# The first 20 microseconds of a GEGLU feed-forward kernel: another order of chunks, two blocks of x transposed by TensorE, and constant matmuls until x lands

## The chip, the cores and the metric

The kernel runs on one core of one Trainium2 chip. The metric is the device time of one execution in microseconds (us). "The span" is the time from the first to the last instruction in the profile, about 1.8 us shorter than the device time.

PE is TensorE, DVE is VectorE, ACT is ScalarE and POOL is GpSimd; SP only issues DMAs here. A q behind a name (SPq, ACTq, PEq) marks the part of the engine that issues its instructions. PSUM is the memory that the matmuls here write to. A constant matmul multiplies constants and its result is thrown away: it only keeps TensorE busy.

Differences here are at most about one per cent, and the rounds ran on different chips, so ratios are taken inside the same rounds. A ratio is the mean time of one kernel's runs over the mean time of the other's runs of the same rounds, so it is not quite the ratio of the medians that are quoted.

## The reference

```
def reference(x, w_gate, w_up, w_down):          # all bfloat16
    return (gelu_tanh(x @ w_gate) * (x @ w_up)) @ w_down
# x: 32*32 = 1024 tokens x 1024;  w_gate, w_up: 1024 x 3584;  w_down: 3584 x 1024
```

Contraction over 1024 is eight blocks of 128 (k = 0 to 7). The 3584 gate and up columns are 28 chunks of 128 (m). The 1024 tokens are two halves of 512 (h). One matmul takes a 128x128 weight block and 512 tokens, and a finished (m, h) pair needs eight of them for gate and eight for up, in two PSUM banks. The eight banks (the program's tile `ps`, 128x8x512) hold four pairs at a time. Work on "one block k" in the head is therefore eight matmuls, in both kernels.

## The kernel before

A small list scheduler writes instructions to each engine in program order and waits for exactly what each one needs. So the order inside one engine's list matters: an engine that waits holds up all that stands behind it in its own list, DMA issues included. The head, abridged:

```
# SP: all of x, transposed by DMA, one 1024x128 block per DMA
for k in range(DK):
    pr.add("sp", "dma_start_transpose", xT[:, k:k + 1, :], xf[:, k * P:(k + 1) * P], w=[("x", k)], dma=f"x{k}")
# ACT: gate and up weights of chunks 0 and 1, two blocks k per DMA (rows of 512 bytes)
for k in range(0, DK, 2):
    load_w("act", "g", 0, k, k + 2)
    load_w("act", "u", 0, k, k + 2)
for i in range(22):                              # constant matmuls, before x lands
    pr.add("pe", "matmul", ps[:, 7, 0:P], scr[:, :], scr[:, :], start=True, stop=True, r=["scr"], w=[("ps", 7)])
# ... further weight loads on SP and ACT ...
KO = DK - 2
units = [(m, h) for m in range(2) for h in range(2)]     # 2 chunks x 2 token halves = 8 banks
for k in range(KO):                              # contraction outermost
    for kind in ("g", "u"):
        for i, (m, h) in enumerate(units):
            mm_gu(kind, m, h, k, 2 * i + (kind == "u"))
# ... blocks 6 and 7 pair by pair, each followed by GELU and the product;
# ... then chunks 2 to 27 one pair at a time, then the down projection (not touched)
```

## Time and profile before

| | before |
|---|---|
| median device time, three runs | 303.19 us |
| span | 301.6 us |
| TensorE (PE) busy | 293.9 us, 97% |
| chain of work that ended last | 94% PE |
| first real matmul starts | 5.84 us |
| 49th real matmul (first one of block 6) starts | 19.21 us |

TensorE bounds the kernel, and what it loses before its last matmul it loses nearly all in the head; copying and storing the last piece, 2.4 us, is not touched. The chain that ended last has the steady rate. Its columns are start, length, and what it was:

```profile
5.67 8.30 DMA xT<-in_x_dram
...
14.02 0.82 PE ps L98 x3
...
14.89 10.74 PE ps L98 x49
...
25.68 10.74 PE ps L98 x49
```

Fifty matmuls of 512 columns take 10.79 us (14.89 to 25.68), 0.216 us each, and it goes on like that until the half-width matmuls of the down projection. The line says x49 because about one record in fifty is missing in this trace: it has 439 of the 448 gate matmuls. Before that, the chain runs through a transposing DMA of x, issued at 5.67 us and landed at 13.97: the fourth block.

A useful yardstick is the start of the 49th real matmul. Without any loss it would start at 48 x 0.2158 = 10.36 us. Whatever it starts later than that is the loss of the head: here 19.21 - 10.36 = 8.85 us.

The timeline of the head shows how the loss arises. Its columns are start, length, engine and instruction, count, and in brackets the idle time before with what ended it. Length includes the tail of the last matmul, and the idle time counts only from the end of that tail, so rates and waits are read from the starts:

```profile
1.00 2.53 PE L98 MATMUL ps<-scr 128*128 128x128 bf16 x22 [1.00 <-POOL scr L98]
...
5.84 1.87 PE L98 MATMUL ps<-xT,wg 128*128 128x512 bf16 x4 [2.32 <-DMA xT<-in_x_dram]
...
7.50 1.91 PE L98 MATMUL ps<-xT,wu 128*128 128x512 bf16 x4
...
9.21 1.51 PE L98 MATMUL ps<-xT,wg 128*128 128x512 bf16 x4
...
10.56 1.03 PE L98 MATMUL ps<-xT,wu 128*128 128x512 bf16 x4
...
11.51 1.02 PE L98 MATMUL ps<-xT,wg 128*128 128x512 bf16 x4
...
14.02 0.82 PE L98 MATMUL ps<-xT,wg 128*128 128x512 bf16 x3 [0.62 <-DMA xT<-in_x_dram]
...
19.21 0.59 PE L98 MATMUL ps<-xT,wg 128*128 128x512 bf16 x2
```

There is a hole from 3.5 to 5.84 us. After it four matmuls take 1.7 us (0.43 us each, half rate) until about 10.3 us, then 0.86 us. A wait for x ends at 14.02. (The trace has three of the four matmuls there.) The last line is the 49th matmul.

One more line is needed for the argument, the group of x's transposing DMAs (duration of the issue: least, median and greatest, in ns):

```profile
L98 SPq DMA_TRANSPOSE xT<-in_x_dram x8: 1235/1358/3987, 0.7 to 15.2; - x8
```

### The profile page before, as it was taken

How to read it: one execution, taken by the hardware profiler on the slowest of the kernel's cores; microseconds unless marked ns; L12 is line 12 of the kernel's file. 1: busy time of each engine (PE TensorE's matmuls, PEld its weight loads, DVE VectorE, ACT ScalarE, POOL GpSimd, SP SyncE). 2: the span in 40 equal slices, each digit the busy share in tenths (PEclk: the TensorE clock that was granted, in tenths of full speed). 3: DMA queues.
4: the chain of work that ended last, by engine and by line, in shares of the span. 5: the costliest groups of instructions: out<-in, count | busy, mean ns of one | idle time of the engine just before them, and what ended most of it. 6: DMA issues, size and time to landing. Idle time of an engine off the chain costs nothing.

```text
span 301.6 us, 3132 instructions
## 1 busy us (share of the span) xinstructions
PE 293.9 (97%) x1368; PEld 136.8 (45%) x1394; DVE 43.8 (15%) x64; ACT 40.1 (13%) x67; POOL 0.4 (0%) x5
## 2 busy tenths in 40 slices
PE   5999999999999999999999999999999999999996
PEld 3344444444444444444444444444444444444455
DVE  0022211112111122111121111220000000000000
ACT  1022112111112111121111211110000000000000
POOL 0000000000000000000000000000000000000000
DMA  8999460302905705603021030000000100010001
GB/s 161 252 254 350 146 230 11 131 0 83 332 4 176 245 0 194 225 9 133 0 86 56 0 139 2 0 0 17 20 17 17 37 17 17 17 37 17 17 17 37
DMA packets 31341, 26.41 MB, mean 88 GB/s; under 512 B 9184, under 2 KB 27744, under 8 KB 31328
## 3 DMA queue, kind: packets, MB, share of 16 engines
q1 hardware_dynamic: 28112, 24.64, 26.5%
q10 hardware_dynamic: 3216, 1.57, 2.4%
q8 instruction: 11, 0.18, 0.3%
q14 instruction: 2, 0.02, 0.0%
HBM read 22.02 MB, written 2.10 MB: 80 GB/s over the span
## 4 chain that ended last, share of the span: by engine, by line
PE 94%; DMA 3%; SPq 2%; issue 1%; ACT 0%
PE ps L98 94%; DMA xT<-in_x_dram 3%; SPq L98 2%; ACT xT L98 0%
## 5 line engine op out<-in xcount | busy, mean ns | idle before, releaser
L98 PE MATMUL ps<-xT,wg 128*128 128x512 bf16 x439 | 107.2, 383 | 3.4 <-DMA xT<-in_x_dram 2.9
L98 PE MATMUL ps<-xT,wu 128*128 128x512 bf16 x439 | 106.9, 381 | 0.5
L98 PE MATMUL ps<-wd,hT 128*128 128x512 bf16 (+1 forms) x468 | 96.5, 366 | 0.4
L98 PEld LDWEIGHTS ps<-xT,wg 128*128 128x128 bf16 x448 | 44.0, 99 | 57.1 <-issue 4.6
L98 PEld LDWEIGHTS ps<-wd,hT 128*128 128x128 bf16 x476 | 46.6, 98 | 50.4
L98 PEld LDWEIGHTS ps<-xT,wu 128*128 128x128 bf16 x448 | 44.0, 98 | 53.5 <-issue 1.1
L98 DVE TENSOR_TENSOR hT<-g,ps 128x512 bf16<-128x512 f32 x56 | 38.5, 688 | 164.6 <-PE ps L98 164.6
L98 ACT ACTIVATE g<-ps 128x512 f32<-128x512 f32 x56 | 33.4, 597 | 165.6 <-PE ps L98 165.6
L98 DVE CAST xT<-ps 128x512 bf16<-128x512 f32 (+1 forms) x8 | 5.3, 658 | 88.1 <-PE ps L98 88.1
L98 ACT ACTIVATE xT<-ps 128x512 bf16<-128x512 f32 (+1 forms) x9 | 5.2, 573 | 93.1 <-PE ps L98 93.1
L98 PE MATMUL ps<-scr 128*128 128x128 bf16 x22 | 2.5, 313 | 1.0 <-POOL scr L98 1.0
L98 PEld LDWEIGHTS ps<-scr 128*128 128x128 bf16 x22 | 2.3, 147 | 1.0 <-POOL scr L98 1.0
L98 ACT ACT_TABLE_LOAD x1 | 1.3, 1283 | 0.7 <-PEq L276 0.7
L98 ACT ACTIVATE warm<-const-float32-0.0 128x1 f32<-128x1 f32 x1 | 0.2, 203 | 0.0
L98 POOL MEMSET scr<- 128x128 bf16 x1 | 0.2, 204 | 0.3 <-POOLq L276 0.3
L276 POOL MEMSET const-bfloat16-1.0<- 128x1 bf16 x1 | 0.1, 102 | 0.0
L276 POOL MEMSET const-uint8-127<- 128x1 uint8 x1 | 0.1, 101 | 0.0
L276 POOL MEMSET const-float32-0.0<- 128x1 f32 x1 | 0.1, 98 | 0.2 <-issue 0.2
L276 POOL MEMSET const-float32-1.0<- 128x1 f32 x1 | 0.1, 98 | 0.0
## 6 DMA issues: line engine op xcount, KB each, us to landing
wd<-in_w_down_dram SPq DMA_DIRECT2D x7, 1024.0 KB, 5.2
wg<-in_w_gate_dram SPq DMA_DIRECT2D x6, 1024.0 KB, 7.7
wu<-in_w_up_dram SPq DMA_DIRECT2D x6, 1024.0 KB, 10.6
out_dram<-xT SPq DMA_DIRECT2D x15, 128.0 KB, 1.7
wg<-in_w_gate_dram ACTq DMA_DIRECT2D x4, 128.0 KB, 5.1
wu<-in_w_up_dram ACTq DMA_DIRECT2D x4, 128.0 KB, 6.1
wu<-in_w_up_dram ACTq DMA_DIRECT2D x1, 512.0 KB, 8.1
wg<-in_w_gate_dram SPq DMA_DIRECT2D x1, 512.0 KB, 5.0
```

The lines of the kernel that those rows point to most:

```text
L98: ins = getattr(eng, name)(*args, **kw)
L276: nc = _bacc.Bacc("TRN2", target_bir_lowering=False, num_devices=1)
```

## The change

Its intent is to start real work earlier, to need less transposed x per block, and to have TensorE at full rate by then.

- The first eight banks hold four chunks by one token half, instead of two chunks by two halves. A block k then needs 512 tokens of x (128 KB instead of 256) and 256 KB of weights (instead of 128), in rows of 1 KB instead of 512 bytes.
- Blocks 0 and 1 of the first token half come by one plain DMA and are transposed by TensorE, and are copied from PSUM by VectorE and ACT.
- All other x still comes by transposing DMA, in 14 halves of 512 tokens.
- The constant matmuls start earlier and are longer, to last until x lands.

```
+        xn = sb("xn", [P, 4, 2 * P], BF16)
-        groups = [(0, 2, 0, 0), (2, 2, 0, 2)]      # then groups of 4 chunks
+        groups = [(c, min(GW, FM - c), (c // GW) % NWB, 0) for c in range(0, FM, GW)]
+        # identity for the transposes: memset and affine_select on POOL
+        for n in [512] * 7 + [128] * 4:
+            pr.add("pe", "matmul", ps[:, 3, 0:n], one[:, 0:P], one[:, 0:n], start=True, stop=True, w=[("ps", 3)])
+        NX = 2
+        pr.add("sp", "dma_start", xn[:, :, :], x_r[:, 0:4, 0:NX * P], w=["xn"], dma="xn")
-        for k in range(DK):
-            pr.add("sp", "dma_start_transpose", xT[:, k:k + 1, :], xf[:, k * P:(k + 1) * P], ...)
+        for h in range(2):
+            for k in range(NX if h == 0 else 0, DK):
+                pr.add("sp", "dma_start_transpose", xT[:, k:k + 1, h * 512:(h + 1) * 512], ...)
+        for k in range(NX):
+            load_w("act", "g", 0, k, k + 1)
+            load_w("act", "u", 0, k, k + 1)
+        for k in range(NX):
+            for i, b in enumerate((6, 7) if k == 0 else (4, 5)):
+                half = ps[:, b, 0:P].bitcast(BF16)
+                for t in range(2):
+                    pr.add("pe", "transpose", half[:, t * P:(t + 1) * P], xn[:, 2 * i + t, k * P:(k + 1) * P], ident[:, :], ...)
+                dst = xT[:, k, i * 256:(i + 1) * 256]
+                if i == 0:
+                    pr.add("dve", "tensor_copy", dst, half, ...)
+                else:
+                    pr.add("act", "activation", dst, half, ACTF.Copy, ...)
-        for k in range(0, DK, 2):
+        for k in range(NX, DK, 2):
             load_w("act", "g", 0, k, k + 2)
             load_w("act", "u", 0, k, k + 2)
-        # 22 constant matmuls of 128 columns; 2 x 2 pairs with contraction outermost
+        # per token half: 4 chunks, contraction outermost, last two blocks chunk by chunk
 ... (the rest follows from the new groups)
```

More of the change, by code (lines that the diff above doesn't have):

```diff
@@ L120, in bass_standalone__geglu_ffn__sampling_kernel @@
     out_r = of.rearrange("(tc p) d -> p tc d", p=P)
+    x_r = xf.rearrange("(tc p) d -> p tc d", p=P)
     wg_r = w_gate.rearrange("(dk p) f -> p dk f", p=P)
@@ L140, in bass_standalone__geglu_ffn__sampling_kernel @@
         warm = sb("warm", [P, 2], FP32)
-        scr = sb("scr", [P, P], BF16)
+        ident = sb("ident", [P, P], BF16)
+        xn = sb("xn", [P, 4, 2 * P], BF16)
         osb = xT
@@ L144, in bass_standalone__geglu_ffn__sampling_kernel @@
         const0 = nc.const_aps.tensor(0.0, [P, 1], FP32)
-        groups = [(0, 2, 0, 0), (2, 2, 0, 2)]
-        c, j = 4, 1
-        while c < FM:
-            n = min(GW, FM - c)
-            groups.append((c, n, j % NWB, 0))
-            c, j = c + n, j + 1
+        groups = [(c, min(GW, FM - c), (c // GW) % NWB, 0) for c in range(0, FM, GW)]
         where = {}
@@ L170, in mm_gu @@
                 start=(k == 0), stop=(k == DK - 1),
-                r=[(kind, buf, slot, k), ("x", k)], w=[("ps", bank)])
+                r=[(kind, buf, slot, k), ("x", k, h)] + ([("x", k, "b")] if h == 0 else []), w=[("ps", bank)])
         glu_n = [0]
@@ L181, in glu @@
                 r=[("gb", g), ("ps", bu)], w=[("h", m, h)])
-        pr.add("pool", "memset", scr[:, :], 1.0, w=["scr"])
-        pr.add("act", "activation", warm[:, 0:1], const0, ACTF.Gelu_apprx_tanh)
-        for k in range(DK):
-            pr.add("sp", "dma_start_transpose", xT[:, k:k + 1, :], xf[:, k * P:(k + 1) * P], w=[("x", k)], dma=f"x{k}")
-        for k in range(0, DK, 2):
+        one = nc.const_aps.tensor(1.0, [P, 512], BF16)
+        pr.add("pool", "memset", ident[:, :], 0.0, w=["id0"])
@@ new lines, in bass_standalone__geglu_ffn__sampling_kernel @@
+        pr.add("pool", "affine_select", ident[:, :], ident[:, :], [[-1, P]], ALU.not_equal, 1.0,
+               base=0, channel_multiplier=1, r=["id0"], w=["ident"])
+        for n in [512] * 7 + [128] * 4:
[4 more added lines that the diff above has]
+            for k in range(NX if h == 0 else 0, DK):
+                pr.add("sp", "dma_start_transpose", xT[:, k:k + 1, h * 512:(h + 1) * 512],
+                       xf[h * 512:(h + 1) * 512, k * P:(k + 1) * P], w=[("x", k, h)], dma=f"x{k}_{h}")
@@ new lines, in bass_standalone__geglu_ffn__sampling_kernel @@
+        pr.add("act", "activation", warm[:, 0:1], const0, ACTF.Gelu_apprx_tanh)
+        for k in range(NX):
[5 more added lines that the diff above has]
+                for t in range(2):
+                    pr.add("pe", "transpose", half[:, t * P:(t + 1) * P], xn[:, 2 * i + t, k * P:(k + 1) * P],
+                           ident[:, :], r=["xn", "ident"], w=[("ps", b)])
+                dst = xT[:, k, i * 256:(i + 1) * 256]
+                if i == 0:
+                    pr.add("dve", "tensor_copy", dst, half, r=[("ps", b)], w=[("x", k, 0)])
+                else:
+                    pr.add("act", "activation", dst, half, ACTF.Copy, r=[("ps", b)], w=[("x", k, "b")])
@@ L189, in bass_standalone__geglu_ffn__sampling_kernel @@
+        for k in range(NX, DK, 2):
             load_w("act", "g", 0, k, k + 2)
             load_w("act", "u", 0, k, k + 2)
-        NDUMMY = 22
-        for i in range(NDUMMY):
-            pr.add("pe", "matmul", ps[:, 7, 0:P], scr[:, :], scr[:, :], start=True, stop=True,
-                   r=["scr"], w=[("ps", 7)])
-        load_w("sp", "g", 1)
-        load_w("act", "u", 1)
-        load_w("sp", "g", 2)
-        load_w("sp", "u", 2)
-        KO = DK - 2
-        units = [(m, h) for m in range(2) for h in range(2)]
@@ L203, in bass_standalone__geglu_ffn__sampling_kernel @@
-        for k in range(KO):
-            for kind in ("g", "u"):
-                for i, (m, h) in enumerate(units):
-                    mm_gu(kind, m, h, k, 2 * i + (kind == "u"))
-        for i, (m, h) in enumerate(units):
-            for kind, b in (("g", 2 * i), ("u", 2 * i + 1)):
-                for k in range(KO, DK):
-                    mm_gu(kind, m, h, k, b)
-            glu(m, h, 2 * i, 2 * i + 1)
+        KO = 2
+        for h in range(2):
+            steps = []
+            for m in range(4):
+                steps += [(m, kind, k) for kind in "gu" for k in range(KO)] if h else []
+            for k in range(KO if h else 0, DK - KO):
+                steps += [(m, kind, k) for kind in "gu" for m in range(4)]
+            for m in range(4):
+                steps += [(m, kind, k) for kind in "gu" for k in range(DK - KO, DK)] + [(m, None, None)]
+            for m, kind, k in steps:
+                if kind is None:
+                    glu(m, h, 2 * m, 2 * m + 1)
+                else:
+                    mm_gu(kind, m, h, k, 2 * m + (kind == "u"))
@@ L214, in bass_standalone__geglu_ffn__sampling_kernel @@
+        for gi in range(1, 3):
+            load_w("sp", "g", gi)
+            load_w("sp", "u", gi)
         wd_pieces = [(a, min(FM, a + 4)) for a in range(0, FM, 4)]
         loaded = 2
-        u = 4
-        for m in range(2, FM):
+        u = 8
+        for m in range(4, FM):
             for h in range(2):
@@ L250, in bass_standalone__geglu_ffn__sampling_kernel @@
                 pr.add("act", "activation", osb[:, tc, col:col + n], ps[:, b, 0:n], ACTF.Copy,
-                       r=[("ps", b)], w=[("o", ji), ("x", tc)])
+                       r=[("ps", b)], w=[("o", ji), ("x", tc, 0), ("x", tc, 1), ("x", tc, "b")])
             else:
                 pr.add("dve", "tensor_copy", osb[:, tc, col:col + n], ps[:, b, 0:n],
-                       r=[("ps", b)], w=[("o", ji), ("x", tc)])
+                       r=[("ps", b)], w=[("o", ji), ("x", tc, 0), ("x", tc, 1), ("x", tc, "b")])
             pr.add("sp", "dma_start", out_r[:, tc, col:col + n], osb[:, tc, col:col + n],
```

## The prediction

> **What bounds the kernel now.** TensorE. The page has PE busy 97%; the chain of waits is 94% PE. In steady state the chain runs 10.79 us per 50 matmuls of 512 columns, 0.216 us each. The work is 896 + 420 such matmuls and 56 of half width, 1344 in all: 290.0 us. The last PE step ends at 299.2, so about 9 us are lost, all at the head. Copying and storing the last piece, 2.4 us, does not change.
>
> The timeline shows that loss: (a) no real matmul until 5.84 us, when the first transposing DMA (1024x128, issued at 0.74) lands; the 22 small constant matmuls ended at 3.5 and PE idled 2.3 us; (b) from 5.84 to 10.3 matmuls start 0.43 us apart, half rate: 2.2 us lost; (c) waits for the third and fourth x block, until 11.5 and 14.0, about 1.2 us. Transposed blocks land at about 5.8, 8.4, 11.4 and 14.0; the work on one takes 8 x 0.216 = 1.73 us at full rate, so x by DMA alone, beside the weights, comes too slowly.
>
> [...] the spacing halves at 10.3, 4.5 us after PE became busy for good.
>
> **What the change does.**
> - x of contraction blocks 0 and 1 (first 512 tokens) comes as one plain 256 KB DMA. With first packets at about 2.05 us and 190 to 285 GB/s shared with block 0's weights, I estimate landing at 4.0 to 4.3 us.
> - Eight TensorE transposes and four PSUM copies of 256 columns follow (512-column copies take 0.57 to 0.66 us; estimate 0.35). First real matmul near 5.1 us.
> - Constant matmuls run from about 0.75 to at most 4.15 us (7 x 0.43 + 4 x 0.11), without the 2.3 us hole. Full rate should come at 5 to 7 us: (b) falls to about 0.4 us.
> - An eight-matmul block needs 128 KB of transposed x instead of 256, but 256 KB of weights instead of 128. The transpose stream (about 1.3 us of issue per 256 KB when unhindered) no longer limits.
> - New risk: weights of blocks 2 to 7 (1.5 MB) are issued by ACT behind its two copies, at about 5.3 us. ACT-queue weights landed 2.7 to 6.5 us after issue before. Gate 2,3 is wanted at about 9, up 2,3 at 9.8. I expect 0 to 2 us of new waits, centre 0.7.
> - Matmul count, down projection, evictions and stores stay.
>
> **Sum.** New head loss 5.1 + 0.4 + 0.7 = 6.2 us against about 9: gain near 2.9 us, all on the critical path because PE never waits later. Predicted 300.3 us, 1% faster, 80% range 299.0 to 301.8. A 2% gain needs a head loss under 3 us, before x can be on chip.
>
> **What would show it.** First xT matmul at 4.8 to 5.4 us; spacing 0.216 us by 7 us; no wait on transposed x in the first 20 us; waits, if any, on weights of blocks 2 to 7; PE chain unbroken afterwards, same spacing.
>
> **What would make it wrong.** [...] The identity from POOL is late. Weights behind ACT's copies arrive after 10 us (+2 us). Half-size transposes cost as much issue as whole ones, and x limits again.
>
> Chances: faster by over 2% 0.02, within 2% 0.96, slower 0.02.

Full rate at 5 to 7 us, and so the 0.4 us, was the estimate. What the trace gives for it is the 4.5 us from 5.84 to 10.3; counted from the start of the constants at 0.75 us, that puts full rate at 5.25.

## The result

| | before | changed |
|---|---|---|
| median device time, four runs each, same rounds | 303.35 us | 301.43 us |
| lowest to highest | 303.04 to 303.69 | 301.04 to 301.60 |
| ratio | | 0.9935 (95% interval 0.9918 to 0.9952) |
| span | 301.6 us | 299.7 us |
| first real matmul | 5.84 us | 5.34 us |
| 49th real matmul | 19.21 us | 17.36 us |
| loss of the head | 8.85 us | 7.00 us |

The kernel became 0.65% faster. The 49th real matmul starts 1.85 us earlier and the median fell by 1.92, so the whole gain is in the head. The timeline of the changed kernel's head:

```profile
0.78 3.57 PE L98 MATMUL ps<-const-bfloat16-1.0 128*128 128x512 bf16 x11 [0.78 <-PEq L296]
...
4.14 1.06 PE L98 MATMUL ps<-ident,xn 128*128 128x128 bf16 x8
...
4.81 0.81 ACT L98 ACTIVATE xT<-ps 128x256 bf16<-128x256 bf16 x2 [2.58 <-PE ps L98]
5.25 0.39 ACTq L98 DMA_DIRECT2D wg<-in_w_gate_dram  x1
...
5.34 1.28 PE L98 MATMUL ps<-xT,wg 128*128 128x512 bf16 x4
...
6.46 1.03 PE L98 MATMUL ps<-xT,wu 128*128 128x512 bf16 x4
...
8.19 1.03 PE L98 MATMUL ps<-xT,wu 128*128 128x512 bf16 x4
...
10.10 1.04 PE L98 MATMUL ps<-xT,wg 128*128 128x512 bf16 x4 [0.88 <-DMA wg<-in_w_gate_dram]
...
11.31 1.04 PE L98 MATMUL ps<-xT,wu 128*128 128x512 bf16 x4 [0.17 <-DMA wu<-in_w_up_dram]
...
17.36 0.59 PE L98 MATMUL ps<-xT,wg 128*128 128x512 bf16 x2
```

The constants pass into the transposes without a hole, x's blocks 0 and 1 are copied, and the first real matmul starts at 5.34 us. Full rate is there by about 6 us instead of 10.3. But block 2's gate weights, issued by ACT only at 5.25 us, land at about 10.05, and its up weights, issued at 5.67, at 11.25. The chain that ended last says the same. It leaves TensorE and goes through ACT's copy to the load of the up weights:

```profile
0.78 4.44 PE ps L98 x19
5.24 0.38 ACT xT L98
5.67 5.58 DMA wu<-in_w_up_dram
11.31 2.33 PE ps L98 x10
```

The loss of 7.00 us can be added up from the starts. The first real matmul starts at 5.34. The first 16 would be done at 9.05 (8.19 + 0.86), 0.26 us more than at full rate. The wait for gate 2 is 1.05 us (9.05 to 10.10), and the wait for up 2 is 0.35 us (10.96 to 11.31). Together that is 7.00. So 1.4 us of the head is a wait that the old kernel did not have. This is one execution; in a second profile of the same kernel (the last experiment below) the two waits come to 0.48 and 0.58 us by the starts, 1.06 in all.

### The profile page after: what moved, and what is told of

Same layout as the page of the kernel before. It is cut to its first block, busy times and chain, and to the rows that moved or that the text cites. A ratio compares the mean times of both kernels' runs of the same rounds, so it can differ in the third digit from the quotient of the medians.

```text
span 299.7 us, 3141 instructions
## 1 busy us (share of the span) xinstructions
PE 294.0 (98%) x1365; PEld 136.3 (45%) x1391; DVE 44.4 (15%) x66; ACT 40.8 (14%) x69; POOL 0.7 (0%) x6
## 4 chain that ended last, share of the span: by engine, by line
PE 96%; DMA 2%; issue 1%; ACT 0%; ACTq 0%
PE ps L98 96%; DMA wu<-in_w_up_dram 2%; ACT xT L98 0%; ACTq L98 0%
## 5 line engine op out<-in xcount | busy, mean ns | idle before, releaser
L98 ACT ACTIVATE xT<-ps 128x512 bf16<-128x512 f32 (+2 forms) x11 | 5.9, 539 | 95.7 <-PE ps L98 95.7
L98 PE MATMUL ps<-const-bfloat16-1.0 128*128 128x512 bf16 (+1 forms) x11 | 3.6, 513 | 0.8 <-PEq L296 0.8
L98 PEld LDWEIGHTS ps<-const-bfloat16-1.0 128*128 128x128 bf16 x11 | 1.4, 143 | 2.7 <-issue 2.7
L98 DVE COPY xT<-ps 128x256 bf16<-128x256 bf16 x2 | 0.6, 292 | 4.7 <-PE ps L98 4.6
L98 PE MATMUL ps<-ident,xn 128*128 128x128 bf16 x8 | 1.1, 314 | 0.0
L98 PEld LDWEIGHTS ps<-ident,xn 128*128 128x128 bf16 x8 | 0.8, 144 | 0.1
```

Of the source, the lines that this page charges most:

```text
L98: ins = getattr(eng, name)(*args, **kw)
```

## The experiments

Each run was checked against the reference and was correct. Times are medians of four to six runs; ratios are to the kernel before in the same rounds. The changed kernel's own ratio in its first rounds was 0.9935.

| experiment | time, us | ratio | loss of the head in the profiled run |
|---|---|---|---|
| weights of blocks 2 and 3 issued before ACT's copies | 300.36 | 0.9895 | 5.73 |
| all four copies on VectorE | 300.23 | 0.9892 | 5.63 |
| transposes not yet needed held back | 301.51 | 0.9931 | 6.66 |
| kernel before, hole filled with constants | 303.78 | 1.0002 | 9.44 |
| changed kernel without constants | 301.77 | 0.9945 | 7.06 |
| copies on VectorE, without constants | 301.58 | 0.9938 | 8.03 |
| copies on VectorE, all x by DMA | 302.64 | 0.9971 | 7.73 |
| copies on VectorE, only block 0 by TensorE | 301.49 | 0.9929 | 6.15 |
| all x by DMA, longer constants | 303.18 | 0.9986 | 8.34 |
| copies on VectorE, longer constants | 300.40 | 0.9896 | 5.94 |
| changed kernel again | 301.89 | 0.9956 | 6.47 |
| copies on VectorE, shorter constants | 301.66 | 0.9936 | 7.74 |

The last column is one execution each and the times are several, so the two columns agree only roughly.

### What made the weights of block 2 late

Two causes were possible. They were issued late, because ACT held them behind its copies (theory A in the expectations below); or the DMA engines were too full to bring them (rival B). The trace shows when these loads were issued: the first of them at 5.25 us, when ACT's second copy started (5.24); the load before it in ACT's list had been issued at 2.50.

**Weights of blocks 2 and 3 issued first.**

```
         for k in range(NX):
             load_w("act", "g", 0, k, k + 1)
             load_w("act", "u", 0, k, k + 1)
+        load_w("act", "g", 0, NX, NX + 2)
+        load_w("act", "u", 0, NX, NX + 2)
         ... transposes and copies ...
-        for k in range(NX, DK, 2):
+        for k in range(NX + 2, DK, 2):
```

> The changed kernel with the gate and up loads of blocks 2 and 3 issued by ACT before its two copies (at about 3.2 and 3.9 us instead of 5.25 and 5.67). Theory A (they were late because ACT issued them behind its copies): they land near 8 and 9.3 us, the two waits of 1.1 and 0.35 us before block 2 vanish, and the time falls from 301.4 to about 300.1. Rival B (the DMA engines are full with transposes and loads, so nothing can land earlier whatever the order of issue): a wait of 1 us or more stays or moves to a later block, 301.2 or more.

Measured: 300.36 us, ratio 0.9895, 0.4% below the changed kernel's 0.9935. The loads were issued at 3.18 and 3.81 us and landed at about 8.5 and 10.0. TensorE's matmuls have no wait from the first block to the last one of the head; block 2 starts at 9.18:

```profile
8.31 1.03 PE L98 MATMUL ps<-xT,wu 128*128 128x512 bf16 x4
9.18 1.03 PE L98 MATMUL ps<-xT,wg 128*128 128x512 bf16 x4
10.04 1.03 PE L98 MATMUL ps<-xT,wu 128*128 128x512 bf16 x4
```

Theory A fits, and the engines were not too full to bring these loads in time. The load of x landed 0.3 us later (4.4 instead of 4.1 us), so the first real matmul moved to 5.62. More weights were on the way: x took 3.7 us from issue to landing, against 3.4 and 3.5 in the two profiles of the changed kernel. That the weights delayed it is likely, but not shown.

**All four copies on VectorE.** ACT then issues all weights without a stop.

```
-                    pr.add("act", "activation", dst, half, ACTF.Copy, r=[("ps", b)], w=[("x", k, "b")])
+                    pr.add("dve", "tensor_copy", dst, half, r=[("ps", b)], w=[("x", k, "b")])
```

> The changed kernel with all four copies on VectorE, so that ACT issues all loads of block 0 to 7 without a stop (last by about 7 us). The second copy is done near 5.25 us as before, so the first real matmul stays at 5.3 to 5.4. Theory A: waits on blocks 2 and 3 vanish, about 300.1 us. Rival B: a wait of 1 us or more stays, on weights or now on transposed x, 301.2 or more.

Measured: 300.23 us, ratio 0.9892, the lowest here, though within the noise of the runs at 0.9895 and 0.9896. The timeline of its head:

```profile
4.47 0.62 PE L98 MATMUL ps<-ident,xn 128*128 128x128 bf16 x8 [0.35 <-DMA xn<-in_x_dram]
...
4.80 0.88 DVE L98 COPY xT<-ps 128x256 bf16<-128x256 bf16 x4 [4.80 <-PE ps L98]
...
5.43 1.02 PE L98 MATMUL ps<-xT,wg 128*128 128x512 bf16 x4 [0.34 <-DVE xT L98]
...
8.02 1.03 PE L98 MATMUL ps<-xT,wu 128*128 128x512 bf16 x4
...
8.88 1.03 PE L98 MATMUL ps<-xT,wg 128*128 128x512 bf16 x4
...
9.94 1.04 PE L98 MATMUL ps<-xT,wu 128*128 128x512 bf16 x4
```

The wait for gate 2 is gone. A wait of 0.2 us for up 2 is left (9.74 to 9.94). VectorE does the four copies in 0.88 us, and the first real matmul needs only the first two of them, so nothing is lost by taking them from ACT.

**Transposes not yet needed held back.** The weights stay behind ACT's copies, but the transposing DMAs of blocks 4 to 7 and of the second token half wait until up 2,3 has landed.

```
-                pr.add("sp", "dma_start_transpose", xT[...], xf[...], w=[("x", k, h)], ...)
+                # blocks 4 to 7 and h = 1 only:
+                pr.add("sp", "dma_start_transpose", xT[...], xf[...], r=[("u", 0, 0, 2)], w=[("x", k, h)], ...)
```

> The changed kernel with the weights issued as late as before (5.25 and 5.67 us), but the transposing DMAs of blocks 4 to 7 and of the second token half held back until up 2,3 has landed. Theory A (late issue alone): gate 2,3 and up 2,3 still land near 9.7 and 11, about 301.3 us. Rival B (they share the DMA engines with transposes not needed yet): they land near 8.5 and 9.2 us, the waits before block 2 vanish, 300.1 us, unless the held x of block 4 (wanted at 12.5 us) then comes late itself, which would show as a wait on transposed x of up to 1 us.

Measured: 301.51 us, ratio 0.9931, no change in time, but the wait moved. The DMA issues of gate 2,3 and up 2,3 (the last column is us from issue to landing), first in the changed kernel:

```profile
wg<-in_w_gate_dram ACTq DMA_DIRECT2D x1, 256.0 KB, 4.8
wu<-in_w_up_dram ACTq DMA_DIRECT2D x1, 256.0 KB, 5.6
```

and with the transposes held back:

```profile
wg<-in_w_gate_dram ACTq DMA_DIRECT2D x1, 256.0 KB, 3.3
wu<-in_w_up_dram ACTq DMA_DIRECT2D x1, 256.0 KB, 3.5
```

Issued at 5.00 and 5.42, they landed in time and block 2 started without a wait, at 8.75. In the second profile of the changed kernel they took 4.2 and 5.2 us, so the gap is beyond that spread. So contention was the other half of the cause: theory A alone (landing near 9.7 and 11) is refuted. Both things are needed for the full wait, and taking away either removes most of it: all of it in the run with the weights first and in this one; with copies on VectorE 0.2 us stays on up 2, and more in a variant with one more transposing DMA (below). Holding x back had its price, as the expectation allowed:

```profile
8.75 1.03 PE L98 MATMUL ps<-xT,wg 128*128 128x512 bf16 x4
...
13.57 1.02 PE L98 MATMUL ps<-xT,wg 128*128 128x512 bf16 x4 [1.21 <-DMA xT<-in_x_dram]
```

TensorE waited for x of block 4 instead. The transposing DMAs are issued by SP and the weights by ACT, and still the ones delayed the others here: the same load took 4.8 us beside all of them, and 3.3 with those held back that were not needed yet.

### What the half rate cost

**The kernel before, with the hole filled.** Five more constant matmuls run after the 22.

```
+        one = nc.const_aps.tensor(1.0, [P, 512], BF16)
+        for i in range(5):
+            pr.add("pe", "matmul", ps[:, 7, :], one[:, 0:P], one[:, :], start=True, stop=True, w=[("ps", 7)])
```

> The kernel before with five more constant matmuls of 512 columns, so that TensorE has no hole from 3.5 to 5.8 us. If x limits its head (the fourth block lands at 14.0 us whatever TensorE does before), the spacing halves earlier but the time stays: 303.0 to 303.5. If the half rate from 5.84 to 10.3 us cost its 2.2 us by itself, 301.0 to 301.5.

Measured: 303.78 us, ratio 1.0002 (0.9988 to 1.0017); the kernel before had 303.75 in these rounds. Its timeline:

```profile
6.78 1.03 PE L98 MATMUL ps<-xT,wu 128*128 128x512 bf16 x4
8.24 1.04 PE L98 MATMUL ps<-xT,wg 128*128 128x512 bf16 x4 [0.43 <-DMA xT<-in_x_dram]
...
11.92 1.02 PE L98 MATMUL ps<-xT,wg 128*128 128x512 bf16 x4 [1.78 <-DMA xT<-in_x_dram]
...
14.61 1.04 PE L98 MATMUL ps<-xT,wg 128*128 128x512 bf16 x4 [0.81 <-DMA xT<-in_x_dram]
```

Full rate came by 6.8 us instead of 10.3, and all of it was given back as waits for x. In the kernel before, the 2.2 us of half rate were hidden behind the transposing DMAs.

**No constants, in the changed kernel and in the version with copies on VectorE.**

```
-        for n in [512] * 7 + [128] * 4:
+        for n in []:
```

> The changed kernel without its eleven constant matmuls. TensorE is then idle until x lands at 4.1 us; the first real matmul stays at 5.3, but at half rate (0.43 us). If the half rate lasts until 7.5 to 11 us, its cost is partly hidden behind the two waits for weights (until 10.1 and 11.3): 0 to 1.3 us more than 301.4, centre 302.0. If the constants did nothing: 301.4.

> The version with all four copies on VectorE (300.2 us, no waits for weights to hide behind), without the constant matmuls. [...] the full cost shows: half rate from 5.4 to between 7.5 and 11 us, 1.0 to 2.8 us more, centre 302.0. If they buy nothing: 300.2.

That half rate would last until 7.5 to 11 us was the estimate in both texts; the traces at hand give one point for it, the 4.5 us of the kernel before, which, counted from x's landing at 4.1 us, would be 8.6.

Measured: 301.77 us (ratio 0.9945 against 0.9935, so about 0.1%, inside the noise) for the changed kernel, and 301.58 us (0.9938 against 0.9892, so 0.46% or 1.4 us) for the version with copies on VectorE. The same constants are worth next to nothing while weights arrive late, and 1.4 us once they do not. In the second run the matmuls of blocks 0 and 1 start 0.42 us apart until about 10.5 us:

```profile
8.93 1.86 PE L98 MATMUL ps<-xT,wg 128*128 128x512 bf16 x4
10.62 1.03 PE L98 MATMUL ps<-xT,wu 128*128 128x512 bf16 x4
```

**Constants that end too early.** The version with copies on VectorE, with only five constants.

```
-        for n in [512] * 7 + [128] * 4:
+        for n in [512] * 5:
```

> The version with copies on VectorE, with the constants cut to five of 512 columns, which end at about 2.9 us, 1.5 us before x lands. [...] 301.3 to 301.8, half rate until 9 us or later. [...] 300.2 to 300.6.

The first range stands for a hole that costs as much as having no constants, the second for a hole that costs little or nothing.

Measured: 301.66 us, ratio 0.9936, as without any constants. The profiled run has a hole of 1.4 us before the transposes and half rate until about 10 us:

```profile
4.44 1.04 PE L98 MATMUL ps<-ident,xn 128*128 128x128 bf16 x8 [1.38 <-DMA xn<-in_x_dram]
...
5.53 1.86 PE L98 MATMUL ps<-xT,wg 128*128 128x512 bf16 x4
```

The times spread from 300.82 to 302.38, so the hole did not cost the same each time. Why, these runs do not show.

**Constants without any hole.** Eight of 512 and two of 128 columns, and two more of 128 between the transposes and the first real matmul.

> The version with copies on VectorE, with the constants lengthened to 4.4 us (8 of 512 and 2 of 128) and two more of 128 columns between the TensorE transposes and the first real matmul, so that no hole is left. First real matmul still near 5.4 us. [...] 300.2, no change. [...] up to 0.3 us less, 299.9, with a smaller spread. If the extra matmuls stand in the way of the first real one: up to 0.3 us more.

300.2 us stands for holes that cost nothing in any run, 299.9 for holes that cost some of the runs time.

Measured: 300.40 us, ratio 0.9896, no gain over 300.23. The first real matmul starts at 5.46 us. So the holes of about 0.35 us that were left cost nothing that these runs can show.

### Whether TensorE had to transpose at all

**All x by DMA.** In the version with copies on VectorE, x of blocks 0 and 1 also comes by transposing DMAs; the weight loads are the same.

```
-        NX = 2
+        NX = 0        # no plain load, no transposes by TensorE, 16 transposing DMAs
         ... (the loops over the weight loads keep their bounds)
```

> The version with copies on VectorE, but without TensorE transposes: all 16 halves of x by transposing DMA, the same weight loads from ACT, the same constants. Theory P (the TensorE transposes are what starts the real work early): the first half block lands at about 4.5 us but the following ones only every 1.2 to 2 us behind it, so TensorE waits for x of blocks 1 to 3, 0.5 to 2 us in all: 300.7 to 302. Rival Q (the order of chunks, which needs half as much transposed x per matmul, did it all): no waits for x, 300.2 or less.

Measured: 302.64 us, ratio 0.9971, slower than either theory expected. Real work started at 5.13 us, no later than with TensorE's transposes. But the constants had ended 0.8 us before, and the matmuls ran at half rate until 9.9 us. That left it open whether x or the rate was to blame, so the constants were made longer.

```
-        for n in [512] * 7 + [128] * 4:
+        for n in [512] * 10 + [128] * 2:
```

> The version with all x by transposing DMA again, but with constants until about 5 us (10 of 512 columns and 2 of 128), because in its first trial TensorE had a hole of 0.8 us before the first real matmul and then ran at half rate until 9.9 us. Theory P (x by DMA comes too slowly: blocks 2, 3 and 4 landed at about 9.8, 12.6 and 14.6 us, wanted at 8.6, 10.3 and 12.0 at full rate): the half rate was hidden, the waits for x now show instead, and the time stays at 302.3 to 302.9. Rival R (it lost only by the half rate): about 300.5.

Measured: 303.18 us, ratio 0.9986, within its interval (0.9971 to 1.0000) barely faster than the kernel before, and 0.3 us above the range that theory P gave. The first matmuls were at full rate at once, and TensorE waited for x before blocks 0, 2, 3 and 4:

```profile
5.80 1.02 PE L98 MATMUL ps<-xT,wg 128*128 128x512 bf16 x4 [0.90 <-DMA xT<-in_x_dram]
...
10.37 1.02 PE L98 MATMUL ps<-xT,wg 128*128 128x512 bf16 x4 [0.96 <-DMA xT<-in_x_dram]
...
12.88 1.04 PE L98 MATMUL ps<-xT,wg 128*128 128x512 bf16 x4 [0.62 <-DMA xT<-in_x_dram]
...
15.24 1.02 PE L98 MATMUL ps<-xT,wg 128*128 128x512 bf16 x4 [0.46 <-DMA xT<-in_x_dram]
```

So theory P's mechanism, waits for x, holds and rival R falls. Against the 0.9892 of the version with two blocks transposed by TensorE, these transposes are worth 0.9%, about 2.9 us. Why is x still late when only half of it is needed? The groups of the transposing DMAs, in the changed kernel:

```profile
L98 SPq DMA_TRANSPOSE xT<-in_x_dram x14: 1174/1262/2740, 1.2 to 20.6; - x14
```

A half costs SP nearly as much issue (1.26 us in the median, 1.17 at least) as a whole block did before (1.36 and 1.24). In the run with longer constants the halves landed at about 5.6, 7.4, 10.2, 12.8 and 15.1 us, hardly closer than the whole blocks before (5.8, 8.4, 11.4, 14.0). And the DMA queues shared differently. Between 5 and 13 us (queue, packets, MB, and the time that its packets took as a share of the time of the 16 engines; the two shares can add up to over 100%), before:

```profile
q10 hardware_dynamic: 2417, 1.19, 72.4%
q1 hardware_dynamic: 2632, 0.66, 51.8%
```

and with all x by DMA and longer constants:

```profile
q10 hardware_dynamic: 1451, 1.40, 82.0%
q1 hardware_dynamic: 1671, 0.40, 29.3%
```

Queue 1 is SP's, with x in packets of about 250 bytes; queue 10 is ACT's, with weights. In both of these runs the two queues moved about as many packets as each other (2417 and 2632, 1451 and 1671). With weight rows of 1 KB instead of 512 bytes, equal packets are a much smaller share for x: 0.40 MB instead of 0.66. Why the counts are so close is not shown. In the changed kernel, whose weights are issued later, the counts in the same stretch are not equal (1278 for weights, 2288 for x), and no run here changed the row size alone. So longer weight rows as the cause of the smaller share is an explanation that fits two runs, not one that is shown. By the landing times, the new order of chunks by itself brought x hardly sooner. What it did, by its construction, was halve the x that a block needs, and the two blocks by TensorE gave the DMA a lead of two blocks, which it kept: once real work has started, the changed kernel's profile has no wait for x. Whether the new order is needed beside the two blocks is open: no run combined TensorE's transposes with the old order.

**Only block 0 by TensorE.**

```
-        NX = 2
+        NX = 1        # plain load of 128 KB, rows of 256 bytes
         ... (xn made smaller, weights of block 1 loaded on their own, all copies on VectorE)
```

> The version with copies on VectorE with only contraction block 0 transposed by TensorE (plain DMA of 128 KB, rows of 256 bytes), block 1 by transposing DMA. The smaller DMA should land about 0.5 us earlier, so the first real matmul at about 4.9 us. If block 1 then lands before 6.6 us, 299.8; if it lands later (the second transposing DMA landed near 7 us), TensorE waits for it and the gain is lost: 300.2 to 300.6.

Measured: 301.49 us, ratio 0.9929, outside both ranges that were expected. The smaller load landed no earlier (3.4 us after issue, as the larger one in the changed kernel), so the premise was wrong: the first real matmul started at 5.27. The profiled run, one of the fastest at 300.68, waits for up 2 (0.65 us of idle time), although ACT issued it without a stop. The six runs spread from 300.64 to 302.62, and no slow one was profiled, so why the median is 1.3 us above that of the version with two blocks stays open.

### The changed kernel again

> The changed kernel again, unedited, for a comparison with the improved version in the same rounds: 301.4, and 1.2 us more than the version with copies on VectorE and filled constants.

Measured in the same rounds as the filled version: median 301.89, ratio 0.9956, with a wide spread of 301.12 to 304.03. The slowest run had a mean granted clock of 0.994, the others 1.000. The filled version's mean is 300.39 and this one's 302.18, 1.8 us apart, or 1.4 us without that one run; expected was 1.2. The waits for gate 2 and up 2 are in its profile again (0.31 and 0.41 us of idle time, 0.48 and 0.58 by the starts). That profile is of the fastest of the six runs, 301.12.

## Why the prediction was right or wrong

The predicted time was 300.3 us with 299.0 to 301.8, and 301.43 was measured, inside the range. "Within 2%" was right. The gain was 1.9 us instead of the expected 2.9, so the mechanism was right in the main and some sizes were off.

| term of the sum | predicted | measured |
|---|---|---|
| loss of the head before | about 9 us | 8.85 |
| first real matmul | 5.1 us | 5.34 |
| left of the half rate | 0.4 us | 0.26 |
| new waits for weights | 0.7 us | 1.40 |
| loss after | 6.2 us | 7.00 |

- **The mis-sized term is "I expect 0 to 2 us of new waits, centre 0.7".** It measured 1.40 us (1.06 in the second profile), inside its range but up to twice its centre, for the two weights and at the place that the prediction named ("gate 2,3 is wanted at about 9, up 2,3 at 9.8"). The listed danger that these weights land after 10 us came true: 10.05 and 11.25. Removing most of the wait gives 300.23 us. That this is nearly the predicted 300.3 is partly luck: the predicted sum still held 0.7 us of waits and 0.4 of half rate, and that version's profile loses 5.63 us, not 6.2.
- **First real matmul at 4.8 to 5.4 us:** right, at 5.34. x landed at 4.1 us as estimated.
- **Spacing 0.216 us by 7 us:** right, from about 6.
- **No wait on transposed x in the first 20 us, waits only on weights of blocks 2 to 7, unbroken afterwards:** right.
- **"(b) ... half rate: 2.2 us lost" and "(b) falls to about 0.4 us", as a gain of its own:** it is no such gain in the kernel before, where filling the hole changed nothing (1.0002). The prediction listed three losses side by side as parts of a sum, and x's arrival stood behind all of them. Its total was nearly right, because the change removed the wait for x at the same time.
- **"The transpose stream ... no longer limits":** right only thanks to the two blocks by TensorE. With all x by DMA in the new order it limits again (303.18 us). The listed danger that half-size transposes cost as much issue as whole ones was real: 1.26 against 1.36 us.
- **The identity from POOL is late:** it was not; it was ready at 1.5 us.
- **A 2% gain is out of reach:** no run contradicts it. The best version here gained 1.1% and still loses 5.6 us at the head, nearly all of it before x is on chip and transposed.

## What to carry to other kernels

When several losses lie one behind another in a head, do not add them up: ask which arrival ends last, and what each becomes when the one behind it is gone. The same constant matmuls were worth nothing in one version and 1.4 us in another. Before giving an engine a small copy, look at what DMA issues stand behind it in its list: moving two copies of 0.4 us from ACT to VectorE gave 0.43%, about 1.3 us. Halving a transposing DMA need not halve its issue time (1.26 against 1.36 us here). Whether longer rows in a plain queue beside it take the engines from it is worth a test; it is not shown here.

## Four more measurements

- In the kernel before, between 14 and 15 us, with only transposing DMAs of x on the DMA engines, they moved 287 GB/s; plain weight loads in the changed kernel between 26 and 28 us moved 358. Those packets are of about 1 KB and x's of about 250 bytes, so the size may be part of it; no run tells the two apart.
- Eight transposes by TensorE took 1.06 us in the changed kernel and 1.04 us with the shorter constants, where the four real matmuls behind them took 1.12 and 1.65 us. They took 0.62 us in the version with copies on VectorE, where the four real matmuls behind them were at full rate (0.86 us). Whether transposes help to bring full rate no run here tells.
- A hole of 0.8 us before full rate was reached (all x by DMA) went with half rate for another 4.8 us, while a hole of 0.9 us after it had been reached (the changed kernel, before block 2) was followed by full rate at once. These are single profiles.
- The half rate at the start does not show in the granted clock of the trace: between 6 and 10 us of the kernel before, with matmuls 0.43 us apart, it reads 1.00.
